# Row maxima of banded attention scores: three bursts of 3, 3 and 2 pairs in one four-bank tile instead of four bursts of two pairs

## The chip, the cores and the metric

The kernel runs on one core of a Trainium2 chip. The metric is the device time of one execution in microseconds (us); the time before is the median of three runs. Engines are called by the profile's names: PE (matrix products; PEld is its weight load), DVE (vector), ACT (activation functions and copies), POOL (elementwise work and selects), SP (DMA issue).

## The reference, cut to what matters

```
xn  = layernorm(x)                                   # x: 2048 x 640
q, k, v = split(xn @ wqkv)                           # 32 heads of 20
s   = where(0 <= i - j < 256, q @ k.T / sqrt(20), -1e9)
p   = softmax(s)
out = x + (p @ v) @ wo + (gelu(xn @ w_gate) * (xn @ w_up)) @ w_down   # hidden size 1728
```

The softmax needs, for every row and head, a maximum over the band of 256 keys (or a number near it) before the exponential is taken. The change concerns how these maxima are computed.

## The kernel before

The time falls into three stages: layer norm, transposes and the first projections (to about 57 us); the attention, mixed with the remaining projections (to about 538 us); and two dense stages (gate and up products, then the output products), which the change does not touch.

**Units and slots.** The attention works in 32 *units* u: a group of 4 heads by a chunk of 512 query rows (c = u % 4). `attention()` (L836) writes the order of PE, ACT, DVE, SP and POOL by hand: an engine runs its instructions in the order in which this loop issues them. Each unit has 14 *slots* (NS). In a slot come, in this order: what was put off to it (`tick`, L827, with `max_end` sorted last), the maxima bursts (`pull_max`), in slot 0 the product with v of the unit before (`av_unit`, L613), in the odd slots below 12 two score pieces (`exp_piece`, L578: pieces 0 and 1 in slot 1, up to 10 and 11 in slot 11), the DVE work that was put off as `late` (`flush`), and *fill steps* (`pull_fill`): matmuls of the remaining projections, RATE/NS = 2.207 of them a slot (2 or 3), the same in every version. A projection is 15 steps, so it ends every 6.8 slots, and the slot in which it ends moves from unit to unit.

**Maxima.** A pair (u, i) of `max_pair` (L508) is 128 query rows of two heads (r = 0 and 1). PE is used as four tiles of 64 by 64 (`tile_position`): two halves h of the rows by two heads, with up to 320 key columns. The result stands in two PSUM tiles `ps_m`, one a head, of the pool `psm` (4 tiles, one bank each). DVE reduces each of them with the mask to one column of `mx` (L537). Eight pairs make a unit; then `negate` writes minus the maxima in two bf16 parts (L546, L547), `max_end` (L551) turns them on PE (`ps_n`, a tile of `psm`), ACT copies them (`mr`, L556), and a DMA on ACT's queue brings them into the rows of `qs` that the score product of the unit after reads. Before, the loop pulls two pairs at slot 0, two more at slot 0 behind `av_unit`, two at slot 5 and two at slot 9, and runs 6 pairs ahead of a unit at its start; pair 7 comes in slot 0's first burst, and `max_end` MXD = 7 slots later, in slot 7.

**Scores.** A piece is one or two matmuls into a tile `ps_e` of the pool `psx` (2 tiles, used in turn), read by ACT's exponential (L594). `av_unit` takes both tiles of the same pool for `ps_o`; ACT copies them out (`ob` L641, then the second copy L642), and pieces 0 and 1 of the unit take them again.

**Work put off.** When a projection ends in slot s, ACT's copy of it (`upper`, L291; or L687 and L688, twice, for a gate) is issued in slot s+1 and the DVE step behind it (`middle`, L287; or `c2`, L693, a slot later) with that slot's `flush`; `c4` and `c5` (L701, L708) are DVE steps of an up product, in the next two slots. The ACT step that follows a DVE step (`lower` L269, `c3` L697) is issued LAG[slot] slots later.

Of the kernel before, what the change touches and what calls it, by code (L numbers as in the profile page):

```python
# [9 lines left out]
F32 = mybir.dt.float32  # L10
# [3 lines left out]
OP = mybir.AluOpType  # L14
PSUM = bass.MemoryType.PSUM
# [12 lines left out]
NEG = -3.0e38  # L28
SR = 3 * DH
QROWS = 64 + SR  # L30
NS = 14
RATE = 30.9
LAST = 8
V1_SLOT = 169
MXD = 7
KSLOT = 9
LAG = 3, 5, 4, 4, 4, 4, 3, 3, 4, 3, 2, 1, 1, 1
NFA = 3
HD = D // 2
HR = 5  # L40
# [27 lines left out]
def block_kernel(ctx, tc, x, wqk, wv, wgu, wdo, wdl, out):  # L68
    nc = tc.nc
# [58 lines left out]
    mask = st1.tile([128, 320], F32, name="mask")  # L128
# [8 lines left out]
    pp = ExitStack()  # L137
    psd = pp.enter_context(tc.tile_pool(name="psd", bufs=2, space=PSUM))
    psx = pp.enter_context(tc.tile_pool(name="psx", bufs=2, space=PSUM))
    psm = pp.enter_context(tc.tile_pool(name="psm", bufs=4, space=PSUM))  # L140

    def ln_load(t, lp):
        xi = lp.tile([128, D], F32, name="xi", tag="xi", bufs=8)
# [63 lines left out]
    def at(slot, fn, *a):  # L207
        acts.setdefault(slot, []).append((fn, a))
# [3 lines left out]
    def late(fn, *a):  # L212
        if now[0] is None or now[0] < NS:
            fn(*a)
        else:
            lates.append((fn, a))

    def flush():
        while lates:
            fn, a = lates.pop(0)  # L220
            fn(*a)

    def lag():
        return 1 if now[0] is None or now[0] < NS else LAG[now[0] % NS]

# [129 lines left out]
    nms = [st1.tile([128, 4, 2, 4, 4], BF, name=f"nm{i}") for i in range(2)]  # L355
# [92 lines left out]
    with tc.tile_pool(name="lp", bufs=1, side="right") as lp:  # L448
# [6 lines left out]
        ps = psd.tile([128, C], F32, name="ps_u", tag="dn")  # L455
# [49 lines left out]

    maxes = {}

    def max_pair(u, i):  # L508
        g, c = divmod(u, NC)
        jj, b = divmod(i, 4)  # L510
        q, k = qs[u % NQ], ks[u % NK]
        if i == 0:
            maxes[u] = ap.tile([128, 4, 4], F32, name="mx", tag="mx")
        pss = [psm.tile([128, 320], F32, name="ps_m", tag="mx") for _ in range(2)]
        n = 320 if c else min(320, 128 * b + 128)

        def quarters(cut):
            for h in range(2):
                part = cut(128 * b + 64 * h - 256, 128 * b + 64 * h + 64)
                for r, ps in enumerate(pss):  # L520
                    if part is not None:
                        kt, col, k0, k1 = part
                        rows, j = slice(64 * r, 64 * r + SR), 2 * r + jj
                        q0 = 128 * b + 64 * h
                        ks_ = kt[rows, j, 0:1].to_broadcast([SR, 64]) if k0 == k1 else kt[rows, j, k0:k1]
                        w = max(64, k1 - k0) if k0 == k1 else k1 - k0
                        nc.tensor.matmul(ps[64 * h:64 * h + 64, col:col + w], q[rows, j, q0:q0 + 64], ks_,  # L527
                                         start=True, stop=True, tile_position=(64 * r, 64 * h))

        if c:  # L530
            quarters(lambda lo, hi: (ks[(u - 1) % NK], 0, C + lo, C) if lo < 0 else None)
        elif b < 2:
            quarters(lambda lo, hi: (k, 320 - n, 0, 64 * b) if 320 - hi > 320 - n else None)
        quarters(lambda lo, hi: (k, max(0, -lo), max(0, lo), hi))
        junk = ap.tile([128, 320], BF, name="junk", tag="junk", bufs=1)
        for r, ps in enumerate(pss):
            nc.vector.tensor_tensor_reduce(out=junk[:, 0:n], in0=ps[:, 320 - n:320], in1=mask[:, 320 - n:320], scale=1.0,  # L537
                                           scalar=NEG, op0=OP.add, op1=OP.max,
                                           accum_out=maxes[u][:, 2 * r + jj, b:b + 1])
        if i == 7:  # L540
            mx = maxes.pop(u)
            nm = nms[u % 2]
            maxes[u] = nm

            def negate():
                nc.vector.tensor_scalar(nm[:, 0, 0], mx, -1.0, None, op0=OP.mult)  # L546
                nc.vector.scalar_tensor_tensor(nm[:, 0, 1], mx, -1.0, nm[:, 0, 0], op0=OP.mult, op1=OP.subtract)  # L547

            late(negate)

    def max_end(u):  # L551
        nm = maxes.pop(u)
        ps = psm.tile([128, 128], F32, name="ps_n", tag="mx")
        nc.tensor.matmul(ps, nm.rearrange("p z a j b -> p (z a j b)"), identb, start=True, stop=True)  # L554
        mr = ap.tile([32, 128], BF, name="mr", tag="mr")
        nc.scalar.activation(mr, ps[0:32], AF.Copy)  # L556
        late(lambda: nc.scalar.dma_start(qs[u % NQ][SR:SR + 2].rearrange("p j t -> p (j t)"), mr))
# [256 lines left out]
    stream = ((u, i) for u in range(NU) for i in range(8))  # L814
    fill = filler()
    debt = [0.0]

    def pull_max(n, slot):
        for _ in range(n):
            x = next(stream, None)  # L820
            if x is None:
                return
            max_pair(*x)
            if x[1] == 7:
                at(slot + (MXD if slot >= 0 else 4), max_end, x[0])

    def tick():  # L827
        todo = [y for t in sorted(t for t in acts if t <= now[0]) for y in acts.pop(t)]
        return sorted(todo, key=lambda y: y[0] is max_end)

    def pull_fill(n):
        debt[0] += n
        while debt[0] > 0:
            debt[0] -= next(fill, 1.0)

    def attention():  # L836
        now[0] = -1
        load_stack(0)
        load_stack(1)
        load_stack(2)  # L840
        for i, (p, k, half) in enumerate((p, k, half) for p in range(NC // 2) for k in range(2) for half in range(2)):
            for j, fn in enumerate(x_sums(p, k, half)):
                m = 10 * i + j
                at(NS * (XS0 + m // XSN) + m % XSN, fn)
        for i in range(12):
            now[0] = i - 13
            for fn, a in tick():
                fn(*a)
            if i == 0:
                pull_max(1, now[0])  # L850
                pull_fill(RAMP)
                pull_max(1, now[0])
                debt[0] -= RAMP
            elif i % 2 == 0 or i == 11:
                pull_max(2, now[0])
            flush()
            pull_fill(2 * RAMP)
        pull_fill(GAP)
        for u in range(NU + 1):
            for i in range(NS):  # L860
                T = now[0] = NS * u + i
                for fn, a in tick():
                    fn(*a)
                if i in (0, 5, 9):
                    pull_max(2, T)
                if i == 0 and u:
                    if u == NU:
                        pull_fill(LAST)
                    av_unit(u - 1)
                    flush()  # L870
                    pull_max(2, T)
                if i % 2 and i < 12 and u < NU:
                    exp_piece(u, i - 1)
                    if i == 1 and u:
                        pull_fill(1)
                        debt[0] -= 1
                    exp_piece(u, i)
                flush()
                if u + 3 < NU and i in (KSLOT, 12):
                    load_stack(u + 3, (int(i == KSLOT),))  # L880
                pull_fill(RATE / NS)
        while acts:
            now[0] += 1
            for fn, a in tick():
                fn(*a)
            flush()
        now[0] = None
        run(fill)
        assert not acts
# [273 lines left out]
    for p in range(NP):  # L1163
        ks_ = list(range(NQD))
        if p > 1:
            ks_ = ks_[4:] + ks_[:4]
# [182 lines left out]
    w = tiles, sums  # L1349
# [28 lines left out]
    for j, f in enumerate(range(NFA, NF - 1)):  # L1378
        end = f + 1 == NF - 1
# [49 lines left out]
        if not end:  # L1429
            w = nxt_w[0], sums  # L1430
# [115 lines left out]
```

## Time and profile before

| what | value |
|---|---|
| time, median of 3 runs | 1040.05 us (1039.83 to 1040.26) |
| the profiled execution's own time | 1039.31 us |
| its span, first to last instruction | 1037.6 us |
| granted PE clock | 1.000 |
| PE / PEld / DVE / ACT / POOL busy over the span | 1031.2 / 834.9 / 741.0 / 526.8 / 383.6 us |
| L537 on DVE: 512 reductions | 242.4 us |
| L527 on PE: 1472 matmuls of the maxima | 63.2 us busy |

A row of a timeline view gives the start, the length, the engine, the line, the operation and its tiles, and how many instructions were merged into it; in brackets stands the idle time of the engine before it and what ended that. Matmuls overlap, so the length of a PE row runs past the start of the next; the time that PE spends on something is best read from start to start. In this text unit u begins with its burst at slot 0: unit 23 at 410.76 us, unit 24 at 424.97 us.

### The profile page before, as it was taken

Reading aid. Unit: us, or ns where it says so; the run is one execution under the profiler, and the core shown is the slowest. Engines: PE = TensorE matmul, PEld = TensorE weight load, DVE = VectorE, ACT = ScalarE, POOL = GpSimd, SP = SyncE. Lnnn points to the kernel's source line nnn. Section 1 sums busy time; section 2 is a strip of 40 time slices with the busy share of each in tenths; the row PEclk is TensorE's granted clock in tenths of the full one; section 3 lists DMA queues with packets and bytes.
Section 4 is the critical chain, followed back from the end, with each engine's and each line's share of the span. In section 5 each row is a group of like instructions: output and inputs, shape, how many; then the busy total and the mean of one; then the engine's idle time right before and its main releaser. Section 6 shows DMA issues by size and latency. Waiting matters only on the chain.

```text
span 1037.6 us, 25574 instructions
## 1 busy us (share of the span) xinstructions
PE 1031.2 (99%) x9396; PEld 834.9 (80%) x9396; DVE 741.0 (71%) x2018; ACT 526.8 (51%) x1120; POOL 383.6 (37%) x623
## 2 busy tenths in 40 slices
PE   9999999999999999999999999999999999999998
PEld 8987666666787666666678888888888999999998
DVE  8755676766656676677636778776556888888887
ACT  4444766766666666676675222233234554333332
POOL 5122788888755877766561111101110000000000
PEclk9999999999999999999999999999999999999999
DMA  6642456564533354343325566682217864433333
GB/s 226 182 144 70 126 152 181 167 189 142 175 102 98 113 159 145 110 145 95 109 71 200 199 230 222 237 265 97 86 55 266 246 243 138 139 127 122 117 121 107
DMA packets 102151, 158.74 MB, mean 153 GB/s; under 512 B 14173, under 2 KB 55261, under 8 KB 102025
## 3 DMA queue, kind: packets, MB, share of 16 engines
q1 hardware_dynamic: 99640, 150.94, 45.8%
q10 hardware_dynamic: 2384, 6.16, 1.8%
q8 instruction: 74, 1.21, 0.5%
q14 instruction: 53, 0.43, 0.1%
HBM read 101.78 MB, written 54.92 MB: 151 GB/s over the span
## 4 chain that ended last, share of the span: by engine, by line
PE 95%; DVE 3%; issue 1%; ACT 0%; DMA 0%; DVEq 0%; ACTq 0%
PE ps_g L990 24%; PE ps L1262 23%; PE ps_d L108 21%; PE ps_e L592 8%; PE ps_v L108 7%; PE ps_o L635 6%; PE ps_m L527 5%; DVE junk L537 2%; PE ps_g L108 1%; PE ps_t L190 1%; PE ps_d L370 1%; DMA xi<-x 0%; DVE xi L169 0%; DVE xl L199 0%; PE ps_n L554 0%
## 5 line engine op out<-in xcount | busy, mean ns | idle before, releaser
L537 DVE CUSTOM_DVE_ANT_0 junk<-ps_m,mask 128x320 bf16<-128x320 f32 (+2 forms) x512 | 242.4, 473 | 133.3 <-PE ps_m L527 75.6
L594 ACT ACTIVATE P<-ps_e 128x512 f32<-128x512 f32 (+2 forms) x384 | 198.8, 573 | 63.1 <-PE ps_e L592 61.6
L1262 PE MATMUL ps<-wb,at 128*128 128x320 f32 x999 | 155.9, 309 | 0.0
L1262 PEld LDWEIGHTS ps<-wb,at 128*128 128x128 f32 x999 | 148.9, 188 | 0.2
L607 POOL TENSOR_SCALAR_AFFINE_SELECT P<-P 128x256 f32<-128x256 f32 (+1 forms) x192 | 94.2, 493 | 69.9 <-ACT P L594 67.9
L592 PE MATMUL ps_e<-qs,ks 124*128 124x128 bf16 (+2 forms) x704 | 118.5, 278 | 0.1
L108 PE MATMUL ps_d<-xh,wqh 128*128 128x512 f32 x310 | 98.7, 421 | 0.0
L108 PE MATMUL ps_d<-xl,wqh 128*128 128x512 f32 x310 | 98.5, 422 | 0.0
L108 PE MATMUL ps_d<-xh,wql 128*128 128x512 f32 x310 | 97.6, 418 | 0.0
L101 POOL TENSOR_TENSOR wql<-wr,wqh 128x640 fp32r<-128x640 f32 x12 | 19.2, 1605 | 195.5 <-PE ps_g L990 150.9
L592 PEld LDWEIGHTS <-ks 124*128 124x128 bf16 x704 | 49.5, 98 | 48.9 <-issue 33.5
L1262 PE MATMUL ps<-wt,at 128*128 128x320 f32 x552 | 88.9, 309 | 0.0
L1262 PEld LDWEIGHTS ps<-wt,at 128*128 128x128 f32 x552 | 82.9, 188 | 0.1
L610 POOL TENSOR_SCALAR_AFFINE_SELECT P<-P 128x512 f32<-128x512 f32 (+1 forms) x144 | 76.5, 539 | 16.3 <-ACT P L594 16.3
L1216 ACT ACTIVATE at<-ss 128x512 fp32r<-128x512 f32 x59 | 37.3, 632 | 81.7 <-DVE ss L1095 81.7
L635 PE MATMUL ps_o<-P,v 64*32 64x320 f32 (+4 forms) x2816 | 74.2, 347 | 0.0
L273 POOL TENSOR_TENSOR pt<-r,pt 128x512 bf16<-128x512 f32 x40 | 46.7, 1167 | 63.5 <-ACT pt L269 63.1
L635 PEld LDWEIGHTS ps_o<-P,v 64*32 64x32 f32 x2816 | 50.9, 106 | 21.5 <-issue 0.9
L527 PE MATMUL ps_m<-ks,qs 60*64 60x320 bf16 (+3 forms) x1472 | 63.2, 260 | 1.4 <-DVE xl L199 0.2
L1019 ACT ACTIVATE hr<-hr 128x512 f32<-128x512 f32 x20 | 12.6, 632 | 102.1 <-DVE hr L993 102.1
L108 PEld LDWEIGHTS ps_d<-xh,wql 128*128 128x128 f32 x310 | 56.0, 189 | 10.2 <-issue 1.3
L108 PEld LDWEIGHTS ps_d<-xh,wqh 128*128 128x128 f32 x310 | 56.0, 189 | 10.1 <-issue 1.6
(197 smaller groups left out, 1980.5 us busy)
## 6 DMA issues: line engine op xcount, KB each, us to landing
hd<-he SPq DMA_DIRECT2D x50, 256.0 KB
hr<-hd SPq DMA_DIRECT2D x48, 256.0 KB
wr<-wgu SPq DMA_DIRECT2D x27, 320.0 KB
qs<-qd SPq DMA_DIRECT2D x64, 120.0 KB
ks<-kd SPq DMA_DIRECT2D x64, 120.0 KB
xi<-x SPq DMA_DIRECT2D x16, 320.0 KB
qs<-qd SPq DMA_DIRECT2D x64, 80.0 KB
ks<-kd SPq DMA_DIRECT2D x64, 80.0 KB
```

The costliest lines, as they stand in the source:

```text
L108: nc.tensor.matmul(ps, a(k), b(k), start=n == 0, stop=n == 3 * nk - 1)
L273: nc.gpsimd.tensor_tensor(out=pt[:, l, :], in0=r, in1=pt[:, 1, :], op=OP.subtract)
L527: nc.tensor.matmul(ps[64 * h:64 * h + 64, col:col + w], q[rows, j, q0:q0 + 64], ks_, start=True, stop=True, tile_position=(64 * r, 64 * h))
L537: nc.vector.tensor_tensor_reduce(out=junk[:, 0:n], in0=ps[:, 320 - n:320], in1=mask[:, 320 - n:320], scale=1.0, scalar=NEG, op0=OP.add, op ...
L592: nc.tensor.matmul(ps[:, col:col + n], k[0:QROWS, j, kc:kc + 128], q[0:QROWS, j, q0:q0 + n], start=True, stop=True)
L594: nc.scalar.activation(pt[:, j, lo:hi], ps[:, lo:hi], AF.Exp, scale=SCALE)
L607: nc.gpsimd.affine_select(out=a, in_=a, pattern=[[0, n], [1, 128]], compare_op=OP.is_ge, fill=0.0, base=0, channel_multiplier=-1)
L610: nc.gpsimd.affine_select(out=a, in_=a, pattern=[[0, n], [-1, 128]], compare_op=OP.is_ge, fill=0.0, base=-1, channel_multiplier=1)
L635: nc.tensor.matmul(os[r][32 * j:32 * j + 32, qa:qb], v[rows, w0_:w0_ + 32], pt[rows, j, col + qa - q0:col + qb - q0], start=r not in begun ...
L990: nc.tensor.matmul(ps, i, j, start=first and n == 0, stop=n == len(work) - 1, skip_group_check=True)
L1216: nc.scalar.activation(hi[:, 3:7], s, AF.Copy)
L1262: nc.tensor.matmul(ps[bank][:, 0:HD], *work[bank][j], start=bank not in begun, stop=final[p, bank] == n and j == len(work[bank]) - 1, skip ...
```

## The change

Once the loop over the units begins, the pool `psm` is closed and a pool with a single tile of four banks (`psw`, tile `both`) takes its place; the bursts of the run-up still use `psm`. A unit's eight pairs come in three bursts (`GROUPS`): 3 at slot 0, 3 at slot 3 and 2 at slot 9. In a burst of three, the pairs stand at columns 0, 320 and 640 of the two halves of the tile; the middle pair crosses the border of two banks, where its matmuls are cut in two (`mul`). DVE's reductions of the third and the first pair are issued with the burst; those of the second are issued after the `flush` of slot 1 (for slot 0) or slot 5 (for slot 3), and `negate` behind them. The second burst of slot 0, behind `av_unit`, is gone. `ps_n` becomes a tile of `psx`, the pool of the scores. Pair 7 now comes in slot 3, so `max_end` is in slot 10. The run-up pulls ten pairs instead of fourteen, and LAG has other values.

```diff
+GROUPS = {0: (3, 1), 3: (3, 2), 9: (2, 0)}
-LAG = 3, 5, 4, 4, 4, 4, 3, 3, 4, 3, 2, 1, 1, 1
+LAG = 3, 3, 3, 5, 4, 3, 4, 3, 2, 5, 4, 3, 2, 1
...
+    def widen():
+        pm.close()
+        wide.append(pm.enter_context(tc.tile_pool(name="psw", bufs=1, space=PSUM, reuse_waits="tile")))
...
+    BANK = 512
+    PLACES = {2: ((0, 1024), (512, 1536)), 3: ((0, 1024), (320, 1344), (640, 1664))}
+
+    def max_group(pairs):
+        if wide:
+            both = wide[0].tile([128, 4 * BANK], F32, name="ps_m", tag="m")
+            todo = [max_pair(u, i, (both, both), base) for (u, i), base in zip(pairs, PLACES[len(pairs)])]
+        else:
+            todo = [max_pair(u, i, [psm.tile([128, 320], F32, name="ps_m", tag="mx") for _ in range(2)], (0, 0))
+                    for u, i in pairs]
+
+        def end():
+            for u, i in pairs:
+                if i == 7:
+                    negate(u)
+
+        if len(pairs) == 3:
+            reduce_pair(*todo[2])
+            reduce_pair(*todo[0])
+            return lambda: [reduce_pair(*todo[1]), end()]
+        for x in todo:
+            reduce_pair(*x)
+        end()
...
+        def mul(r, h, kt, col, k0, w):
+            rows, j, q0 = slice(64 * r, 64 * r + SR), 2 * r + jj, 128 * b + 64 * h
+            col += bases[r]
+            while w:
+                m = min(w, BANK - col % BANK)
+                ks_ = kt[rows, j, 0:1].to_broadcast([SR, m]) if k0 is None else kt[rows, j, k0:k0 + m]
+                nc.tensor.matmul(pss[r][64 * h:64 * h + 64, col:col + m], q[rows, j, q0:q0 + 64], ks_,
+                                 start=True, stop=True, tile_position=(64 * r, 64 * h))
+                col, w, k0 = col + m, w - m, k0 if k0 is None else k0 + m
...
-            late(negate)
+    def negate(u):
+        mx = maxes.pop(u)
+        nm = maxes[u] = nms[u % 2]
...
     def max_end(u):
         nm = maxes.pop(u)
-        ps = psm.tile([128, 128], F32, name="ps_n", tag="mx")
+        pool, tag = (psx, "ex") if wide else (psm, "mx")
+        ps = pool.tile([128, 128], F32, name="ps_n", tag=tag)
...
+        rest_ = max_group(pairs)
+        if rest_:
+            at_end[slot + GROUPS[slot % NS][1]] = rest_
+        for u, i in pairs:
+            if i == 7:
+                at(slot + (MXD if wide else 4), max_end, u)
...
-            elif i % 2 == 0 or i == 11:
+            elif i % 2 == 0 and i < 10:
                 pull_max(2, now[0])
...
         pull_fill(GAP)
+        widen()
         for u in range(NU + 1):
             for i in range(NS):
...
-                if i in (0, 5, 9):
-                    pull_max(2, T)
+                if i in GROUPS:
+                    pull_max(GROUPS[i][0], T)
                 if i == 0 and u:
...
                     av_unit(u - 1)
                     flush()
-                    pull_max(2, T)
...
                 flush()
+                if T in at_end:
+                    at_end.pop(T)()
```

More of the change, by code (lines that the diff above doesn't have):

```diff
@@ L139, in block_kernel @@
     psx = pp.enter_context(tc.tile_pool(name="psx", bufs=2, space=PSUM))
-    psm = pp.enter_context(tc.tile_pool(name="psm", bufs=4, space=PSUM))
+    pm = pp.enter_context(ExitStack())
+    psm = pm.enter_context(tc.tile_pool(name="psm", bufs=4, space=PSUM))
+    wide = []
+    def widen():
+        pm.close()
+        wide.append(pm.enter_context(tc.tile_pool(name="psw", bufs=1, space=PSUM, reuse_waits="tile")))
     def ln_load(t, lp):
@@ L506, in block_kernel, with max_pair @@
     maxes = {}
-    def max_pair(u, i):
+    BANK = 512
[18 more added lines that the diff above has]
+        end()
+    def max_pair(u, i, pss, bases):
         g, c = divmod(u, NC)
@@ L513, in max_pair @@
             maxes[u] = ap.tile([128, 4, 4], F32, name="mx", tag="mx")
-        pss = [psm.tile([128, 320], F32, name="ps_m", tag="mx") for _ in range(2)]
         n = 320 if c else min(320, 128 * b + 128)
+        def mul(r, h, kt, col, k0, w):
[7 more added lines that the diff above has]
+                col, w, k0 = col + m, w - m, k0 if k0 is None else k0 + m
         def quarters(cut):
@@ L519, in quarters @@
                 part = cut(128 * b + 64 * h - 256, 128 * b + 64 * h + 64)
-                for r, ps in enumerate(pss):
+                for r in range(2):
                     if part is not None:
                         kt, col, k0, k1 = part
[L523 to L528, printed above, removed]
+                        if k0 == k1:
+                            mul(r, h, kt, col, None, 64)
+                        else:
+                            mul(r, h, kt, col, k0, k1 - k0)
         if c:
@@ L534, in max_pair, with reduce_pair @@
         quarters(lambda lo, hi: (k, max(0, -lo), max(0, lo), hi))
+        return maxes[u], jj, b, n, pss, bases
+    def reduce_pair(mx, jj, b, n, pss, bases):
         junk = ap.tile([128, 320], BF, name="junk", tag="junk", bufs=1)
[L536 to L547, printed above, removed]
-            late(negate)
+        for r in range(2):
+            nc.vector.tensor_tensor_reduce(out=junk[:, 0:n], in0=pss[r][:, bases[r] + 320 - n:bases[r] + 320],
+                                           in1=mask[:, 320 - n:320], scale=1.0, scalar=NEG, op0=OP.add, op1=OP.max,
+                                           accum_out=mx[:, 2 * r + jj, b:b + 1])
+    def negate(u):
+        mx = maxes.pop(u)
+        nm = maxes[u] = nms[u % 2]
+        nc.vector.tensor_scalar(nm[:, 0, 0], mx, -1.0, None, op0=OP.mult)
+        nc.vector.scalar_tensor_tensor(nm[:, 0, 1], mx, -1.0, nm[:, 0, 0], op0=OP.mult, op1=OP.subtract)
     def max_end(u):
         nm = maxes.pop(u)
-        ps = psm.tile([128, 128], F32, name="ps_n", tag="mx")
+        pool, tag = (psx, "ex") if wide else (psm, "mx")
+        ps = pool.tile([128, 128], F32, name="ps_n", tag=tag)
         nc.tensor.matmul(ps, nm.rearrange("p z a j b -> p (z a j b)"), identb, start=True, stop=True)
@@ L816, in block_kernel @@
     debt = [0.0]
+    at_end = {}
     def pull_max(n, slot):
[L819 to L825, printed above, removed]
+        pairs = [x for x in (next(stream, None) for _ in range(n)) if x]
+        if not pairs:
+            return
+        rest_ = max_group(pairs)
[4 more added lines that the diff above has]
+                at(slot + (MXD if wide else 4), max_end, u)
     def tick():
```

## The prediction

> **What bounds the kernel now.** First the page's head, its busy times, and its chain of work by engine.
>
> ```profile
> span 1037.6 us, 25574 instructions
> PE 1031.2 (99%) x9396; PEld 834.9 (80%) x9396; DVE 741.0 (71%) x2018; ACT 526.8 (51%) x1120; POOL 383.6 (37%) x623
> ...
> PE 95%; DVE 3%; issue 1%; ACT 0%; DMA 0%; DVEq 0%; ACTq 0%
> ```
>
> PE sets the end: whatever lengthens or shortens PE's order moves the time one for one. But busy does not mean that it streams: a matmul that waits inside a burst counts as busy. So I read PE's timeline from start to start, in unit 23.
>
> ```profile
> 410.76 0.37 PE L527 MATMUL ps_m<-ks,qs 60*64 60x64 bf16 x12
> 411.06 2.45 PE L635 MATMUL ps_o<-P,v 64*32 64x320 f32 x96
> 413.44 0.47 PE L527 MATMUL ps_m<-ks,qs 60*64 60x320 bf16 x8
> 413.83 0.50 PE L108 MATMUL ps_d<-xh,wqh 128*128 128x512 f32 x1
> ...
> 416.04 0.61 PE L592 MATMUL ps_e<-qs,ks 124*128 124x128 bf16 x4
> ...
> 417.52 0.47 PE L527 MATMUL ps_m<-ks,qs 60*64 60x256 bf16 x16
> 417.93 0.61 PE L592 MATMUL ps_e<-qs,ks 124*128 124x256 bf16 x4
> ...
> 421.05 0.47 PE L527 MATMUL ps_m<-ks,qs 60*64 60x320 bf16 x8
> 421.44 0.61 PE L592 MATMUL ps_e<-qs,ks 124*128 124x128 bf16 x4
> 421.76 0.53 PE L108 MATMUL ps_d<-xh,wql 128*128 128x512 f32 x1
> 422.13 0.85 PE L108 MATMUL ps_d<-xl,wqh 128*128 128x512 f32 x3
> 422.82 0.63 PE L592 MATMUL ps_e<-qs,ks 124*128 124x128 bf16 x4
> ...
> 424.97 0.30 PE L527 MATMUL ps_m<-ks,qs 60*64 60x256 bf16 x4
> ```
>
> A burst of two pairs takes 0.39 to 0.41 us (413.44 to 413.83), with 8 matmuls or with 16. A unit takes 14.21 us. Units with fewer columns in av_unit show something else; here are the first and the last of eight alike (units 1, 5, ... 29), and the longest and the shortest of six other late bursts:
>
> ```profile
> 101.37 0.92 PE L527 MATMUL ps_m<-ks,qs 60*64 60x320 bf16 x8
> 102.22 0.50 PE L108 MATMUL ps_d<-xh,wql 128*128 128x512 f32 x1
> ...
> 497.37 0.92 PE L527 MATMUL ps_m<-ks,qs 60*64 60x320 bf16 x8
> 498.22 0.73 PE L108 MATMUL ps_d<-xl,wqh 128*128 128x512 f32 x2
> ...
> 377.83 0.86 PE L527 MATMUL ps_m<-ks,qs 60*64 60x320 bf16 x8
> ...
> 363.92 0.65 PE L527 MATMUL ps_m<-ks,qs 60*64 60x320 bf16 x8
> ```
>
> Burst to next step is 0.85 there, not 0.39: the second pair waits until DVE has reduced the first burst. So 0.46 us and a slower entry of 0.05 are lost eight times, 4.0 us, and 0.2 to 0.4 six more times, 1.6 together: **5.6 us** of waiting on DVE inside "busy".
>
> DVE's and ACT's rows give what such a wait consists of:
>
> ```profile
> 413.81 0.49 DVE L537 CUSTOM_DVE_ANT_0 junk<-ps_m,mask 128x320 bf16<-128x320 f32 x1 [0.25 <-PE ps_m L527]
> 414.45 0.49 DVE L537 CUSTOM_DVE_ANT_0 junk<-ps_m,mask 128x320 bf16<-128x320 f32 x1
> ...
> 420.25 0.68 DVE L701 TENSOR_TENSOR gs<-ps_d,gs 128x512 f32<-128x512 f32 x1
> 421.04 0.69 DVE L708 SCALAR_TENSOR_TENSOR he<-he,gs 128x512 f32<-128x512 f32 x1
> ...
> 497.82 0.08 DVE L537 DVE_READ_ACCUMULATOR2_ANT mx<- 128x1 f32 x1
> ```
>
> Reductions follow at 0.64 us (413.81 to 414.45); a unit's sixteen are 10.2 of its 14.2 us. The first starts 0.37 after its burst's start, since it waits for the first pair alone. The reduction that unit 29's late pair waited for ended at 497.90, and that pair began at 497.37 + 0.14 + 0.46 = 497.97: a release takes some 0.05 to 0.07.
>
> **The change part by part.**
>
> *Bursts.* Where no burst follows av_unit, as in unit 31, the next step starts as soon as the burst did:
>
> ```profile
> 522.51 2.45 PE L635 MATMUL ps_o<-P,v 64*32 64x320 f32 x96
> 524.89 0.96 PE L108 MATMUL ps_d<-xl,wqh 128*128 128x512 f32 x3
> 525.69 0.39 PE L592 MATMUL ps_e<-qs,ks 124*128 124x128 bf16 x2
> ```
>
> (2.38 us after av_unit's start, as 411.06 to 413.44.) So dropping slot 0's second burst saves 0.39 a unit. Its pairs join other bursts. A pair's columns cost 0.14: score matmuls of 256 columns follow at (0.61 - 0.28)/3 = 0.11 us in the row at 417.93, and 320 columns are 1.25 times that. Net 0.39 - 0.28 = 0.11 us, 29 times: 3.2; the two dropped bursts of the run-up about 0.2 each. **-3.6 us.** The Trainium skill (TensorEngine Tiling (Array Packing), Key Properties) says that a change of tiling mode drains PE; the 0.11 agrees with that, two changes becoming one. The cut matmuls of the middle pairs are 4 more a burst: between 0 and 0.01 us by the x16 and x8 rows, 0.2 at most in all. A reduction across the border of two banks is in no row; two short reductions would be 0.15 dearer at most, nothing excludes it, and I take 0, as it stays one instruction over the same columns.
>
> *Old DVE waits.* The wait of the second burst in slot 0 goes with the burst: **-5.6 us**, if no other takes its place. What is late next is the four parts below.
>
> *The cover of the copies behind av_unit.* Scores 0 and 1 reuse the two tiles that ob and its neighbour read.
>
> ```profile
> 524.97 0.60 ACT L641 ACTIVATE ob<-ps_o 128x512 f32<-128x512 f32 x1 [1.94 <-PE ps_o L635]
> ```
>
> In unit 31, with 3 fill steps, score 0 starts at 525.69, 0.12 after ob's end. With 2 fill steps (0.23 each: three in the 0.69 from 422.13 to 422.82) it would start 0.23 earlier, 0.11 before that end; with 0.05 for the release PE would wait 0.16. Of units 1 to 29 twelve have 2 steps there and a long av_unit (0.16), four 2 steps and a short one (0.2), and units 13 to 17, with shorter steps, 0.7 together: **+3.4 us**.
>
> *ps_n in the scores' ring.* It takes the tile of score 8, and is issued in slot 10, behind 2 or 3 fill steps of slot 9.
>
> ```profile
> 419.95 0.25 ACT L556 ACTIVATE mr<-ps_n 32x128 bf16<-32x128 f32 x1
> ...
> 421.94 1.08 ACT L594 ACTIVATE P<-ps_e 128x512 f32<-128x512 f32 x2 [0.78 <-PE ps_e L592]
> ```
>
> Slot 9's two steps begin at 421.76 and 422.13, so slot 10 would begin at 422.36; ACT has read score 8 after 0.60 (as in ob's row) of the 1.08 for two, at 422.54. So PE stands until 422.59, 0.22 us. By the order of the rows, unit by unit, nineteen units have 2 steps there (4.2); the others lose 0.2 on average where ACT is late (1.2); the present wait of score 11 for score 9 goes (1.0). **+4.4 us.** Behind the wait stand slot 10's fill steps and scores 10 and 11.
>
> *mr behind ACT's other work.* Score 11 takes ps_n's tile, so it waits for mr. mr (0.25) is last in slot 10's tick. If ACT has nothing else there, it runs from 423.0 (the end of score 9's row) to 423.25; score 11 is due two fill steps and score 10 after 422.59, at 422.59 + 0.46 + 0.25 = 423.3, so just later. With a step in between it doesn't:
>
> ```profile
> 267.44 0.63 ACT L269 ACTIVATE pt<-r 128x512 bf16<-128x512 f32 x1
> ...
> 493.03 0.61 ACT L687 ACTIVATE gs<-ps_d 128x512 f32<-128x512 f32 x1
> 493.50 0.62 ACT L688 ACTIVATE he<-ps_d 128x512 f32<-128x512 f32 x1
> ```
>
> By the new LAG (middle in slots 6, 7, 8) `lower` falls into slot 10 in units 10 to 12 and 18 to 20: 0.5 (0.63 less its overlap with the next row) less 0.1, six times. The gate's pair falls there in units 28 to 30: 0.95 (twice the 0.47 from 493.03 to 493.50) less 0.1, three times; upper with a weight copy in units 5 and 6 about 1.0; v copies in 14 and 15 about 0.35. **+7.5 us.** mr's DMA, moved from slot 7 to slot 10, still has five slots before score 0 of the next unit; on ACT's queue scores 10 and 11 stand behind its issue, and nobody waits for them before av_unit.
>
> *One tile for all bursts.* A burst's first matmul now waits for all reductions of the burst before. DVE starts on a burst of three at 0.37 + 0.28 = 0.65, and with nothing between, the sixth reduction frees the tile at 0.65 + 5 x 0.64 + 0.55 = 4.4 us (0.55: its 0.49 and a release). PE comes back at slot 3 after 5.2 (410.76 to 416.04, less 0.39, plus 0.14, plus the 0.16 above), and from slot 3 to slot 9 after 5.0 (416.04 to 421.05 is 5.01; a burst and ps_n leave, a longer burst comes). So 0.6 to 0.8 are spare, and DVE steps issued before the last two reductions eat them. *Slot 0 to 3:* in units 10, 11, 12 and 18 upper stands behind the copies of av_unit on ACT, and middle behind upper:
>
> ```profile
> 244.06 0.47 PE L527 MATMUL ps_m<-ks,qs 60*64 60x320 bf16 x8
> ...
> 245.11 0.61 ACT L291 ACTIVATE pt<-ps_d 128x512 bf16<-128x512 f32 x1
> ...
> 248.32 0.68 DVE L287 TENSOR_TENSOR r<-ps_d,pt 128x512 f32<-128x512 f32 x1
> ...
> 246.68 0.61 PE L592 MATMUL ps_e<-qs,ks 124*128 124x128 bf16 x4
> ```
>
> From av_unit's end (244.06): upper is done at 1.66, middle takes 0.68, two reductions 0.64 + 0.55: 3.5; PE is there at 2.62 - 0.39 = 2.2. Loss 1.3, 1.3, 1.3 and 1.1 (unit 18, 2 steps): 5.0. Unit 0 has no av_unit to cover the reductions (1.5), and units 21 and 25 have c2 with a short one (0.4 each). **+7.2 us.** *Slot 3 to 9:* c4 and c5 lie both in slots 3 to 5 in units 26 to 29 and take 0.68 + 0.69 = 1.4: 0.8 each; one step (0.69) lies there in nine more, 0.1 each. **+4.1 us.** *Slot 9 to 0:* two pairs are freed after 0.37 + 3 x 0.64 + 0.55 = 2.8, PE comes after 3.9: nothing.
>
> **Sum.** -9.2 + 3.4 + 4.4 + 7.5 + 7.2 + 4.1 = +17.4; where a slot has a third fill step (one in five), 0.23 are covered that I counted, about 1.2 in all: +16.2. The profiled execution took 1039.31 us (span 1037.6, 1.7 around it), the median of the runs is 0.74 above: 1039.31 + 16.2 + 0.74 = **1056 us**.
>
> **Rivals.** *Faster: the waits find cover.* If none of the last four parts shows (ACT and DVE reach their rows sooner than by my spacing, because PE, waiting once, lets them catch up), -9.2 + 3.4 gives 1034, and without the 3.4 too 1031. For it: PE's order is shorter in any case. Against: each wait starts from a PE event a few steps before, so an earlier one doesn't help it. It decides once all new waits together stay below 9.2 us. *The ring alone waits:* 3.4 + 4.4 against 9.2, 1039, no change. For it: those two hang on neither LAG nor the projections' phase. Against: the rows at 245.11 and 493.03 lie where they must for the others. *DVE becomes the bound in every unit.* Sixteen reductions (10.2), three other steps (0.7 each) and the three stretches at a burst's start with nothing to reduce (0.65, 0.65, 0.37) are 14.0, with negate's small rows more than the unit's 14.2; in the units shortened by av_unit it is 0.5 over. At 0.35 to 0.5 a unit beyond what I count it gives 1066 to 1070. The Trainium skill (TensorEngine Tiling (Array Packing), PSUM Bottleneck) has it so: faster tiled products can leave the PSUM copy as the limit. By that rule the tile's single copy would be the bound in each unit. Against: DVE steps between the groups fill those stretches. *Not doing what it says:* three bursts whose parts wait singly would keep the 3.6; that is inside the range.
>
> **How the numbers follow.** Forecast 0.62, waits covered 0.16, ring alone 0.12, DVE the bound 0.10. A measurement tells 0.2% (2 us) from no change: faster 0.16, same 0.12, slower 0.72. The forecast alone with half or all of its queue waits is 1044 to 1064; with the neighbours the range is 1036 to 1068, the lower end leaving out most of the first rival.
>
> **What would show it.** Right: ps_m rows stretched at slot 3 in units 10 to 12, at slot 9 in 26 to 29; ps_n 0.2 behind the last fill step; mr as what score 11 waits for; score 0 at ob's end. Wrong: bursts of three at 0.55 us throughout, or first matmuls of a burst that start before the last reduction of the one before.

## The result and the profile after

The changed kernel takes 1058.74 us (median of 4 runs, 1057.96 to 1059.38) against 1040.15 beside it: 1.0177 times as long, 95% interval 1.0161 to 1.0193, or 18.6 us more. The page of its profiled execution, head and chain by engine:

```profile
span 1057.2 us, 25650 instructions
PE 1034.8 (98%) x9644; PEld 841.9 (80%) x9644; DVE 742.0 (70%) x2018; ACT 527.3 (50%) x1120; POOL 384.0 (36%) x623
...
PE 84%; ACT 4%; DVE 4%; DMA 3%; POOL 2%; issue 2%; SPq 0%; ACTq 0%; POOLq 0%; DVEq 0%
```

PE is busy for 3.6 us more, the span is 19.6 longer: most of the loss is idle PE. The chain that ended last was 95% PE and is now 84%; other engines stand in it. The view of the waits (engine, line and releaser: total, times, longest) had no row in which PE waits for DVE or ACT in the attention before; now it has three:

```profile
PE ps_m L553 <- DVE mx L578: 7.3, 9, 1.4
PE ps_e L630 <- ACT mr L594: 4.1, 7, 1.3
PE ps_n L592 <- ACT P L632: 1.4, 1, 1.4
```

These are only the waits long enough to show as idle time. (A fourth row, 0.5 us, names a DMA, `kd<-pt`.) So I also took the start times of `av_unit` and of scores 0, 1, 2, 8, 10 and 11 in units 1 to 31, and subtracted before from the other kernel, stretch by stretch (us, summed; e1 to e12 are the experiments below):

| PE's stretch (us against before) | after | e1 | e2 | e3 | e4 | e9 | e11 | e12 |
|---|---|---|---|---|---|---|---|---|
| `av_unit` | 0.6 | 0.2 | 0.6 | 0.2 | 0.9 | 0.0 | 0.1 | 0.8 |
| its end to score 0 | -12.4 | -11.4 | -12.4 | -10.5 | 0.1 | -12.4 | -10.6 | -10.5 |
| score 0 to 1 | 0.5 | 0.6 | 0.5 | 0.5 | 0.0 | 0.5 | -0.1 | 0.0 |
| score 1 to 2 (slots 1 to 3) | 23.5 | 23.3 | 18.4 | 18.5 | 0.0 | 23.2 | 13.5 | 13.6 |
| score 2 to 8 (slots 3 to 9) | -14.5 | -14.7 | -16.0 | -15.2 | -1.1 | -9.0 | -11.9 | -27.6 |
| score 8 to 10 | 11.0 | 1.9 | 11.5 | 1.9 | 10.7 | 0.2 | 0.3 | 19.5 |
| score 10 to 11 | 5.9 | 0.2 | 5.4 | 0.2 | 4.9 | 0.1 | 0.6 | -0.4 |
| score 11 to `av_unit` | 4.2 | 10.2 | 4.3 | 10.2 | 0.4 | 4.1 | 4.1 | 11.7 |
| sum | 18.7 | 10.3 | 12.3 | 5.7 | 15.8 | 6.6 | -4.0 | 6.9 |

(Another 0.2 to 0.7 is lost ahead of unit 1. The values are of the profiled executions, which lie up to 2.7 below the medians given below.) Bursts that change slots move time between rows, so a row is read against its neighbour: slot 3's burst of three adds 0.63 a unit to slots 1 to 3, and 0.56 leave slots 3 to 9. What is left over is waiting. The timeline of the changed kernel shows four places of it (start, length, engine, line, operation; in brackets the idle time before it):

```profile
168.94 0.39 PE L630 MATMUL ps_e<-qs,ks 124*128 124x128 bf16 x2
169.23 0.60 ACT L298 ACTIVATE pt<-ps_d 128x512 bf16<-128x512 f32 x1 [0.43 <-DMA kd<-pt]
169.72 0.73 ACT L707 ACTIVATE wqh<-wr 128x640 fp32r<-128x640 f32 x1
170.35 0.25 ACT L594 ACTIVATE mr<-ps_n 32x128 bf16<-32x128 f32 x1
170.65 0.38 PE L630 MATMUL ps_e<-qs,ks 124*128 124x128 bf16 x2 [1.31 <-ACT mr L594]
...
236.44 1.19 POOL L280 TENSOR_TENSOR pt<-r,pt 128x512 bf16<-128x512 f32 x1
236.62 0.60 ACT L298 ACTIVATE pt<-ps_d 128x512 bf16<-128x512 f32 x1
...
237.66 0.69 DVE L294 TENSOR_TENSOR r<-ps_d,pt 128x512 f32<-128x512 f32 x1 [2.24 <-POOL pt L280]
238.27 0.48 DVE L578 CUSTOM_DVE_ANT_0 junk<-ps_m,mask 128x320 bf16<-128x320 f32 x1
...
238.79 0.49 DVE L578 CUSTOM_DVE_ANT_0 junk<-ps_m,mask 128x320 bf16<-128x320 f32 x1
239.21 0.08 DVE L578 DVE_READ_ACCUMULATOR2_ANT mx<- 128x1 f32 x1
239.34 0.61 PE L553 MATMUL ps_m<-ks,qs 60*64 60x128 bf16 x20 [1.40 <-DVE mx L578]
...
420.06 0.77 PE L109 MATMUL ps_d<-xh,wql 128*128 128x512 f32 x2
420.24 1.09 ACT L632 ACTIVATE P<-ps_e 128x512 f32<-128x512 f32 x2 [0.72 <-PE ps_e L630]
420.89 0.22 PE L592 MATMUL ps_n<-identb,nm 128*128 128x128 bf16 x1
420.92 0.94 PE L109 MATMUL ps_d<-xl,wqh 128*128 128x512 f32 x3
421.70 0.61 PE L630 MATMUL ps_e<-qs,ks 124*128 124x128 bf16 x4
...
423.63 0.52 PE L553 MATMUL ps_m<-ks,qs 60*64 60x320 bf16 x18
424.08 2.45 PE L673 MATMUL ps_o<-P,v 64*32 64x320 f32 x96
...
426.54 0.60 ACT L679 ACTIVATE ob<-ps_o 128x512 f32<-128x512 f32 x1 [2.31 <-PE ps_o L673]
427.19 0.38 PE L630 MATMUL ps_e<-qs,ks 124*128 124x128 bf16 x2
```

- 168.94 to 170.65 (unit 5): score 11 waits for `mr` (ends 170.60), which stands behind `upper` and a weight copy in ACT's order.
- 236.62 to 239.34 (unit 10, slot 3): `upper` ends at 237.22 and `middle` starts 0.44 later. Its row names POOL: the step at L280 reads the `r` of the projection before, of which there is one buffer, until 236.44 + 1.19 = 237.63, and `middle` writes it. (In units 11, 12 and 18 the row names ACT's `upper` instead, as the prediction has it, and `middle` follows it by 0.1; there the burst waits 1.1 to 1.2, here 1.4.) The middle pair's two reductions stand behind `middle`, and the burst starts 0.05 after the second (239.21 + 0.08).
- 420.06 to 420.89 (unit 22, slot 10): ACT reads score 8 until 420.24 + 0.60 = 420.84; `ps_n` starts 0.05 later. 0.22 of that is idle inside the row of fill steps, so no bracket shows it. The three fill steps behind `ps_n` take 0.78 (420.92 to 421.70), where three took 0.69 before (422.13 to 422.82).
- 426.54 to 427.19: score 0 starts 0.05 after `ob`'s end (427.14).

### The profile page after: what moved, and what is told of

It reads as the page before. It is cut to its first block, busy times and chain, and to the rows that moved or that the text cites. A ratio compares the mean times of both kernels' runs of the same rounds, so it can differ in the third digit from the quotient of the medians.

```text
span 1057.2 us, 25650 instructions
## 1 busy us (share of the span) xinstructions
PE 1034.8 (98%) x9644; PEld 841.9 (80%) x9644; DVE 742.0 (70%) x2018; ACT 527.3 (50%) x1120; POOL 384.0 (36%) x623
## 4 chain that ended last, share of the span: by engine, by line
PE 84%; ACT 4%; DVE 4%; DMA 3%; POOL 2%; issue 2%; SPq 0%; ACTq 0%; POOLq 0%; DVEq 0%
PE ps_g L1034 23%; PE ps L1306 22%; PE ps_d L109 14%; PE ps_v L109 6%; PE ps_e L630 6%; PE ps_o L673 5%; PE ps_m L553 4%; ACT P L632 2%; DVE junk L578 2%; PE ps_g L109 1%; DMA qd<-pt 1%; POOL P L645 1%; DMA qs<-mr 1%; DMA qs<-qd 1%; PE ps_t L197 1%
## 5 line engine op out<-in xcount | busy, mean ns | idle before, releaser
L109 PE MATMUL ps_d<-xl,wqh 128*128 128x512 f32 x310 | 100.7, 423 | 0.0
L280 POOL TENSOR_TENSOR pt<-r,pt 128x512 bf16<-128x512 f32 x40 | 46.8, 1170 | 72.2 <-ACT pt L276 72.2
L553 PEld LDWEIGHTS <-qs 60*64 60x64 bf16 x1720 | 33.9, 106 | 40.2 <-issue 33.8
L109 PEld LDWEIGHTS ps_d<-xl,wqh 128*128 128x128 f32 x310 | 55.5, 189 | 9.3 <-issue 0.4
```

The source lines that it names most:

```text
L109: nc.tensor.matmul(ps, a(k), b(k), start=n == 0, stop=n == 3 * nk - 1)
L280: nc.gpsimd.tensor_tensor(out=pt[:, l, :], in0=r, in1=pt[:, 1, :], op=OP.subtract)
L553: nc.tensor.matmul(pss[r][64 * h:64 * h + 64, col:col + m], q[rows, j, q0:q0 + 64], ks_, start=True, stop=True, tile_position=(64 * r, 64 ...
```

## The experiments

Two questions were open: is it the ring (the two tiles of the scores' pool, used in turn), the shared tile, or only both together; and does a wait that is taken away stay away? Each run has its own runs of the kernel before beside it.

**e1: `ps_n` three slots later.** `-MXD = 7` `+MXD = 10`: slot 13, where the next score is 0 of the unit after.

> The changed kernel with max_end three slots later (MXD = 10: slot 13 in place of slot 10), nothing else. Slot 13 lies two slots behind the last scores, so ps_n finds its tile read, and no score takes its tile after it. Theory (each new wait costs PE by itself): the trace of the changed kernel shows 9 us more between score 8 and score 10 than before beside ps_n itself, and 6 us more between scores 10 and 11; both go, about -13 to -15 us, 1044 to 1046, and ps_n's rows stand without an idle entry for ACT. Rival (DVE and its one tile set the pace, the ring's waits only fill time in which PE would wait anyway): PE then meets the bursts earlier and waits there, less than 5 us saved, over 1053.

Measured: 1050.8 us, ratio 1.0103 (1.0088 to 1.0118): 7.9 less, between the two. The table says why: 14.7 go between scores 8 and 11, and 6.0 come back between score 11 and `av_unit`. Of these some 4 are `ps_n` itself: it stands between fill steps in slot 13 too, and costs 0.12 to 0.14 in nearly every unit. The other 2 are waits in units 2, 5, 6 and 26 to 30, in part for the exponentials of scores 10 and 11 (0.4 in unit 5). Another 1 comes back ahead of score 0, most of it in unit 2, where the row names the DMA of `mr`.

**e2: the middle pair reduced with its burst.**

```diff
-            return lambda: [reduce_pair(*todo[1]), end()]
+            reduce_pair(*todo[1])
+            end()
+            return
```

> The changed kernel with the second pair of a burst of three reduced with the burst, behind the third and the first, and not after the flush one or two slots later; negate follows it. Theory: middle, c4 and c5 no longer stand ahead of the last two reductions, so the late bursts at slot 3 (units 0, 10, 11, 12, 18: 6.3 us in all) and at slot 9 (units 8, 24, 26 to 29: 2.9 us) start on time: -8 to -9 us, about 1050. Rival (the deferred order was needed: middle and the gate's steps come later, projections' tiles come free later): half of it or more comes back as waits of the fill steps or of ACT, over 1054.

Measured: 1052.34 us, ratio 1.0121 (1.0104 to 1.0138): 6.4 less, between the two, 5.1 of it in slots 1 to 3. Unit 10's slot 3 in its timeline:

```profile
236.84 0.08 DVE L580 DVE_READ_ACCUMULATOR2_ANT mx<- 128x1 f32 x1
...
237.37 1.00 PE L109 MATMUL ps_d<-xh,wqh 128*128 128x512 f32 x3
238.07 0.69 DVE L294 TENSOR_TENSOR r<-ps_d,pt 128x512 f32<-128x512 f32 x1 [1.16 <-POOL pt L280]
238.31 0.61 PE L555 MATMUL ps_m<-ks,qs 60*64 60x128 bf16 x20
```

The sixth reduction is over at 236.92, before `middle`, and the burst follows its fill steps with no wait. In units 10, 11, 12 and 18 the late burst came from the *put-off* reductions behind `middle`, not from the single tile alone. Unit 0's wait (1.1) stays, and some of the rival shows: in unit 7 a fill step now waits 1.0 for `middle`.

**e3: both.**

> Both edits: max_end in slot 13 and all reductions with the burst. Theory (waits add up): -22 us, 1036 to 1038, a little below the kernel before; of what was lost only the copies behind av_unit (3.4 us) remain. Rival (DVE bound: waits only change their place): over 1044.

Measured: 1047.09 us, ratio 1.0068 (1.0053 to 1.0083): 11.7 less, where the two alone make 14.3 and the theory had 22. The time is above the rival's 1044, but most of the loss is gone, so the waits do not only change their place. In units 25 to 27 a new wait shows. Timeline of e3:

```profile
442.05 0.62 ACTq L597 DMA_DIRECT2D qs<-mr  x1
...
445.77 0.39 PE L632 MATMUL ps_e<-qs,ks 124*128 124x128 bf16 x2 [0.93 <-DMA qs<-mr]
```

`mr`'s rows reach `qs` some 3 us after the end of their issue (442.67), and score 0 is there first: in these three units slot 13 is too late for the transpose.

**e4: the kernel before with the ring alone.** `ps_n` in the pool of the scores and MXD = 10; bursts, tiles and LAG of before.

```diff
-        ps = psm.tile([128, 128], F32, name="ps_n", tag="mx")
+        pool, tag = (psx, "ex") if now[0] >= NS else (psm, "mx")
+        ps = pool.tile([128, 128], F32, name="ps_n", tag=tag)
```

> The kernel before with one part of the change alone: from unit 1 on ps_n takes a tile of the scores' pool and max_end comes in slot 10 (MXD = 10, as pair 7 is pulled at slot 0); bursts, tiles of the maxima, LAG as before. Theory: about 0.27 us a unit behind score 8 (8 us) and 3 to 6 us between scores 10 and 11 where ACT has other work in slot 10 (fewer lower steps fall there with the old LAG): 1050 to 1054. Rival (the ring costs only together with the shared tile): below 1044.

Measured: 1055.53 us, ratio 1.0149 (1.0134 to 1.0165): 15.9 more, 1.5 above the theory, and in the same two rows of the table as in the changed kernel. The same place in its timeline:

```profile
418.78 0.77 PE L108 MATMUL ps_d<-xh,wql 128*128 128x512 f32 x2
418.95 1.09 ACT L595 ACTIVATE P<-ps_e 128x512 f32<-128x512 f32 x2 [0.82 <-PE ps_e L593]
419.60 0.22 PE L555 MATMUL ps_n<-identb,nm 128*128 128x128 bf16 x1
```

Score 8 is read until 418.95 + 0.60 = 419.55, and `ps_n` follows by 0.05. Alone, the ring costs 15.9 of the 18.6, which would leave about 3 us for the three bursts in one tile. Taken from the other side, e9 below leaves the ring out and still finds 7.4 more than before: the two costs do not simply add, but the ring is the larger by either count.

**e5, e6, e7: `ps_n` out of the ring.** The last burst of a unit leaves columns free in the four-bank tile. e5 writes `ps_n` there, behind slot 9's burst; e6 adds e2's edit; e7 also moves 0.8 of a fill step from slot 1 to slot 0.

```diff
+            both = last_[0] = wide[0].tile([128, 4 * BANK], F32, name="ps_m", tag="m")
...
-        pool, tag = (psx, "ex") if wide else (psm, "mx")
-        ps = pool.tile([128, 128], F32, name="ps_n", tag=tag)
+        if wide:
+            ps = last_[0][:, 320:448]
...
+        if wide and slot % NS == 9 and ends:
+            max_end(ends.pop())
```

> The changed kernel with ps_n taken out of the scores' ring: it is written into 128 free columns of the four-bank tile, right behind slot 9's burst of two pairs, so scores 8, 10 and 11 wait for nobody but the exponentials. Theory (the ring costs what it cost alone in the kernel before, some 16 us, all of it between scores 8 and 11): the 11.0 us between scores 8 and 10 and the 5.9 between scores 10 and 11 go, ps_n's own 0.066 a unit (2 us) comes back behind slot 9's burst: 1058.7 - 16.9 + 2 = 1043.9 us, 1042 to 1046. Rival (a wait taken away is found again at the next burst, since DVE is late for it): the reductions freed by waiting PE make slot 3's and slot 9's bursts later, and it comes out above 1049.

> As e5, and the middle pair of a burst of three reduced with the burst in place of two slots later. Theory: the 6 us that this alone was worth in the changed kernel come on top, 1043.9 - 6.4 = about 1037.5 us (1036 to 1040). Rival (the two are partly the same wait, as the two edits of the first four runs were, which together gave 2.6 less than their sum): above 1041.

> As e6, and 0.8 of a fill step a unit moved from slot 1 to slot 0, so that nearly every unit has three fill steps between av_unit and score 0. Theory (score 0 waits for the copy ob because its cover went with slot 0's second burst, 3.4 us in all): score 0 starts without a wait, 3 us less than e6, about 1034.5. Rival (the wait moves: scores 0 and 1 come as late, or slot 3's burst comes earlier by what was saved and waits for DVE): within 1 us of e6.

Measured: 1137.75, 1129.49 and 1124.82 us, ratios 1.0931 (1.0905 to 1.0958), 1.0855 (1.0839 to 1.0871) and 1.0845 (1.0783 to 1.0906). 66 to 79 us more than the changed kernel: far above the rivals' bounds too, and by a mechanism that neither theory nor rival has. The row of the waits of e5:

```profile
PE ps_m L596 <- DVE mx L580: 66.5, 30, 2.9
```

A case of it in e5's timeline:

```profile
457.82 0.47 PE L555 MATMUL ps_m<-ks,qs 60*64 60x256 bf16 x16
...
460.40 0.08 DVE L580 DVE_READ_ACCUMULATOR2_ANT mx<- 128x1 f32 x1
460.54 0.27 PE L596 MATMUL ps_m<-identb,nm 128*128 128x128 bf16 x1 [2.25 <-DVE mx L580]
460.60 1.06 PE L634 MATMUL ps_e<-qs,ks 124*128 124x128 bf16 x4
461.20 1.73 PE L109 MATMUL ps_d<-xh,wql 128*128 128x512 f32 x3
```

My edit issued `ps_n` behind the four reductions of the same burst, so it waited for the last of them, though it writes other columns (460.54 is 0.06 after that one's end, 460.40 + 0.08): 2.2 us a unit, in 30 units. And what follows is slow: three fill steps behind a score take 1.54 us from start to start (461.20 to the next row's 462.74), where they usually take 0.83 (0.37 and twice 0.23, as at 421.76).

**e8: LAG of before in the changed kernel.**

> The changed kernel with the kernel before's values of LAG, that is only the slots of ACT's steps lower and c3 behind DVE's. Theory (the waits hang on the shared tile and the ring, not on LAG; the late mr of units 5, 6 and 28 to 30 comes from steps that LAG doesn't move): within 2 us of the changed kernel's 1058.7. Rival (as the prediction has it, the new LAG puts lower into slot 10, ahead of mr, in units 10 to 12 and 18 to 20): 2.4 us or more faster.

Measured: 1058.09 us, ratio 1.0178 (1.0159 to 1.0196): no difference clear of the noise. In units 10, 11 and 18 the wait of score 11 gets 0.1 to 0.3 shorter, 0.7 together, so LAG's part in the cost is small at most.

**e9, e10, e11: the same three, with `ps_n` ahead of the reductions.**

```diff
             todo = [max_pair(u, i, (both, both), base) for (u, i), base in zip(pairs, PLACES[len(pairs)])]
...
+        if wide and slot % NS == 9 and ends:
+            max_end(ends.pop(), both[:, 320:448])
```

and in e11

```diff
-                pull_fill(RATE / NS)
+                pull_fill(RATE / NS + (MORE if i == 0 and u else -MORE if i == 1 and u else 0))
```

> As e5, but ps_n and mr are issued ahead of the reductions of slot 9's burst, so that ps_n waits for the negated maxima alone and no longer for the four reductions that follow it in e5 (66.5 us of waiting there in 30 units, with slower matmuls behind each wait). Theory (with that wait gone, the ring's cost of some 16 us is what is left out): 1058.7 - 16.9 + 2 = 1043.9 us, 1042 to 1046. Rival (what the ring took is found again as later bursts): above 1049.

> As e9, with the middle pair of a burst of three reduced with its burst. Theory: 6.4 less, about 1037.5 us (1036 to 1040). Rival (the same wait in part): above 1041.

> As e10, with 0.8 of a fill step a unit moved from slot 1 to slot 0. e7 against e6 gave 4.7 less with the PE order of those two; theory (the copies' cover): 3 to 4 us less than e10, about 1034, and so below the kernel before's 1040. Rival: within 1 us of e10, not below the kernel before.

Measured: 1047.67, 1040.77 and **1037.12** us, ratios 1.0073 (1.0060 to 1.0087), 1.0003 (0.9994 to 1.0012) and 0.9974 (0.9964 to 0.9984). The timeline of e9, slot 9 of unit 22:

```profile
409.81 0.36 PE L557 MATMUL ps_m<-ks,qs 60*64 60x64 bf16 x12
410.11 0.23 PE L596 MATMUL ps_m<-identb,nm 128*128 128x128 bf16 x1
410.17 0.60 PE L634 MATMUL ps_e<-qs,ks 124*128 124x128 bf16 x4
```

Here `ps_n` costs 0.06 and nobody waits. Against the changed kernel 16.6 us go between scores 8 and 11 and 5.5 come back in slots 3 to 9: about 2.0 of `ps_n` itself, and most of the other 3.5 is `ps_n` waiting for `nm`, the negated maxima that it turns (1.07 in unit 30). The waits of e9 have a row for it:

```profile
PE ps_m L596 <- DVE nm L590: 2.8, 5, 1.1
```

So 1047.7 stands between theory and rival, 1.7 above the one and 1.3 below the other, and what comes back is for the most part not the later burst that the rival names. e10 and e11 take 6.9 and 3.7 off, as expected, from a start that is 3.8 higher than expected; e10 is thus level with the kernel before. e11 is 0.3% faster than it; the head of its page:

```profile
span 1034.2 us, 25654 instructions
```

**e12: e11 with the last burst in slot 10.** `-GROUPS = {0: (3, 1), 3: (3, 2), 9: (2, 0)}` `+GROUPS = {0: (3, 1), 3: (3, 2), 10: (2, 0)}`, and `ps_n` goes to slot 10 with it.

> As e11, with the burst of two pairs (and ps_n behind it) in slot 10 in place of slot 9, behind the fill steps of slot 9 and ahead of those of slot 10. In e11 some 3.5 us are still lost at slot 9, where the burst waits for the reductions of slot 3's burst (most in units 6 to 8). Theory (that loss is DVE's lateness against PE by the clock of a unit, so one slot, about 1.0 us, covers it, and two pairs need only 2.8 of the 2.9 us then left to slot 0): about 2.5 us less than e11, 1034.5. Rival (slot 0's burst has no cover left and waits in its turn, or mr's rows land too late for score 0): the same as e11 or slower.

Measured: 1049.39 us, ratio 1.0095 (1.0078 to 1.0112): 12.3 slower than e11. The waits in e11 that it was to cover were not bursts: `ps_n` waits for `nm` in units 6 and 8 (0.9), and a fill step of unit 7 waits 1.6 for `middle`. The first are gone in e12, the second stays (1.5). Slot 0's burst waits in its turn, as the rival has it: the stretch from score 11 to `av_unit` takes 7.6 more than in e11, and another 3.5 are lost between scores 2 and 10 (1.3 in unit 9, where score 10 waits for an exponential). The waits of e12 have a row that was small in e11 (1.4 us, once):

```profile
PEld L560 <- DVE mx L585: 17.1, 28, 1.7
```

(A burst's weight load waits ahead of its first matmul.) But the cause is not the spacing that I costed. Unit 5's end in the timeline of e12:

```profile
167.30 0.23 PE L599 MATMUL ps_m<-identb,nm 128*128 128x128 bf16 x1
...
167.82 0.60 ACT L299 ACTIVATE pt<-ps_d 128x512 bf16<-128x512 f32 x1 [0.17 <-DMA kd<-pt]
168.31 0.73 ACT L714 ACTIVATE wqh<-wr 128x640 fp32r<-128x640 f32 x1
168.94 0.25 ACT L601 ACTIVATE mr<-ps_m 32x128 bf16<-32x128 f32 x1
...
169.22 0.49 DVE L585 CUSTOM_DVE_ANT_0 junk<-ps_m,mask 128x320 bf16<-128x320 f32 x1 [3.21 <-ACT mr L601]
...
171.38 0.61 PE L560 MATMUL ps_m<-ks,qs 60*64 60x320 bf16 x20 [1.26 <-DVE mx L585]
```

DVE's first reduction starts 0.03 after `mr`'s end (169.19), not after the burst (167.30): in this tile the reductions stand behind ACT's copy, and the same 0.03 shows in nearly every unit of e11 and e12. In slot 10 ACT has `upper` and a weight copy ahead of `mr` in units 5 and 6, and the gate's pair in units 28 to 30, the same units where the changed kernel's score 11 waited for it. These five make 4.0 of the 7.6; the rest is 0.2 to 0.6 each in ten other units. The Trainium skill (PSUM — Partial Sum Buffer, Terms) counts two engines on one bank and quadrant at once as an error, reads against reads included; the rows agree, since `mr` and the first pair lie in one bank and do not overlap here. A place for `ps_n` in a bank that no reduction reads first was not tried.

## Why the prediction was right

Slower by 15.9 was forecast, slower by 18.6 came, by the mechanisms named. That the sum is only 2.7 off is partly luck: against a span that grew by 19.6, three terms are too low by 4.6, 1.3 and 1.2, and three others too high by 1.6, 0.9 and 1.2. The sizes, in the order of its parts:

- **Bursts and old DVE waits** (-9.2): near. All waits below make 27.5 (3.4 as forecast, then 9.0 + 5.9 + 6.3 + 2.9 as measured), the span grew by 19.6: leaves -7.9. The bursts are as costed: ahead of `av_unit` three pairs take 0.45 (423.63 to 424.08) where two took 0.30 (410.76 to 411.06), so the third adds 0.15, where 0.14 was taken. Behind slot 0 the stretch to score 0 is 12.4 shorter, where 29 times 0.39, the 5.6 and the 3.4 make 13.5.
- **The cover of the copies** (+3.4): right. In units 3 to 9, 18, 19 and 23 to 29, with two fill steps, score 0 follows the last matmul of `av_unit` by 0.88 (long) or 0.99 (short), 0.05 after `ob`'s end. e11, which gives nearly every unit a third step, is 3.65 below e10.
- **`ps_n` in the ring** (+4.4): right in kind, half its size; this term is what the forecast lacked. The 0.22 behind two fill steps is there to the hundredth (420.89). But scores 8 to 10 take 11.0 more, which is 9.0 without the 2.0 of `ps_n` that moved, and not 5.4: unit 9 loses 1.35 beyond the others, where ACT comes late to score 8, and `ps_n` is dearer in slot 10 than in slot 7. There it cost 0.066 ahead of a score; here it stands between fill steps and costs 0.12 (420.89 to 420.92, and the three steps behind it take 0.09 more). That is 0.05 a unit, 1.5 in all. The units with a third step lose about as much as the others. The 1.0 let go for score 11's old wait didn't go.
- **`mr` behind ACT's other work** (+7.5): 5.9. Units 5 and 6 lose 1.5 and 0.9 where about 1.0 was costed, units 28 to 30 0.6 to 0.8 each where it was 0.85. Behind `lower` 0.4 was costed six times; 0.1 to 0.3 showed, and with the LAG of before (e8) it goes in three of the six.
- **One tile, slot 0 to 3** (+7.2): 6.3. Units 10, 11, 12 and 18 lose 1.1 to 1.5 (5.1 against 5.0), unit 0 1.2 against 1.5; units 21 and 25 nothing. e2 shows the cause in the four, since with the reductions issued at once their wait is gone. The good fit of the 5.0 hides two errors: POOL holds `middle` in unit 10, which the prediction hasn't, and the reductions are quicker than it took them (last point).
- **One tile, slot 3 to 9** (+4.1): 2.9, of which unit 8's 0.5 is a wait for a DMA that e1, e2 and e8 do not have; units 26 to 29 lose 0.4 to 0.7 where 0.8 was costed. **Slot 9 to 0**: nothing, as forecast.
- The **1.2** taken off for third fill steps did not show.
- **The spacing of the reductions**, 0.64 in all these sums, holds only for the kernel before (413.81 to 414.45). In the one tile they follow at 0.52 to 0.53 (238.27 to 238.79), as in every version with it, while e4, with the old tiles, keeps 0.64. A unit's sixteen are thus 8.5 us and not 10.2. No run shows why; it is one reason why both terms of the one tile were too large.

Of the rivals, *waits find cover* fell: the new waits make 24, not less than 9.2, and in e1, e3 and e9 a wait that is taken away partly comes back further on. *The ring alone waits* named the largest part but priced it too low: alone (e4) the ring costs 15.9, of which 10.7 stand at `ps_n`, where it had 4.4, and 4.9 at `mr`, which it left out; and e2 finds 6.4 outside the ring. *DVE the bound in every unit* fell: the plain units (1, 2, 13, 17, 21, 25) are as fast as before or faster, and at 0.53 a reduction its 14.0 us a unit become 12.2. One sentence of the working was too strong: that the shared tile's waits must be where ACT's rows lie. They must be only while two reductions are put off. The working of the range has a slip: the forecast with all of its queue waits is 1056 itself, and nothing in it leads to 1064; the time that came, 1058.7, is above the full sum.

## What to carry to other kernels

A small matmul that borrows a tile of a busy ring pays twice: it waits for the reader before it, and the next user waits for its own copy; price both ends, and try the borrowing alone. Free columns of a tile that is idle in that moment cost 0.06 here in place of some 0.5 a unit, if the matmul is issued *ahead* of the reads of that tile (e5 against e9), what it reads is ready (e9) and its own reader is not late (e12). Reductions that free the only copy of a tile are better issued at once than behind other steps of their engine: worth 6.4 and 6.9 us here (e2, e10), net of a step that then comes later itself.

## What the runs showed of the hardware

A wait of some 2.2 us on PE once a unit costs more than itself. Windows of e5 around the wait of 458 to 460.5 (the stretch and its length, busy us of PE, PEld, DVE, ACT and POOL with the instructions, then the granted clock, DMA share and GB/s):

```profile
457.00:459.00 2.00, 1.29 (x20) 0.77 (x20) 1.86 (x6) 0.89 (x2) 1.04 (x2) 1.00 0.40 122
459.00:461.00 2.00, 0.46 (x3) 0.32 (x3) 1.42 (x6) 0.16 (x1) 0.56 (x1) 0.86 0.72 243
461.00:463.00 2.00, 2.00 (x7) 1.69 (x6) 0.00 (x0) 1.20 (x3) 0.46 (x2) 0.50 0.17 44
463.00:465.00 2.00, 2.00 (x10) 1.27 (x10) 0.00 (x0) 0.86 (x2) 0.67 (x2) 0.79 0.32 99
465.00:467.00 2.00, 2.00 (x55) 1.17 (x60) 0.66 (x3) 1.21 (x3) 1.71 (x4) 1.00 0.55 132
...
200.00:540.00 340.00, 290.81 (x3967) 209.17 (x3967) 184.38 (x698) 188.10 (x424) 207.13 (x353) 0.95 0.39 115
```

The granted clock falls to 0.50 while PE has work again, and is back at 1.00 in the stretch from 465; hence the slow fill steps at 461.20. The mean from 200 to 540 us is 0.95 (last row). e5 takes 90 us more than e9 by the medians; the waits of its row are 66.5 of it, and the clock is about the size of the rest: by my estimate from the 0.95, some 480 us of attention take 25 longer. In the changed kernel, with waits up to 1.4, the mean over the execution stays at 0.999. The Trainium skill (TensorE: Matmul & The Clock Gate, What's actually happening) has these two states, half clock and full, and lets the clock fall after an idle window of about 3.4 us; the 0.50 agrees, while here it fell at the end of 2.25 us of idle PE.
